# Batch 1 of a linear-attention and gated-MLP kernel: the first q division on GpSimd, the first v casts on ScalarE and VectorE, both q transposes ahead of the kv products

## The chip, the cores and the metric

The kernel runs on one core of a Trainium2 chip. The metric is the device time of one execution in microseconds; lower is better.

Names: TensorE (PE in the profile, PEld for its weight loads), VectorE (DVE), ScalarE (ACT), GpSimd (POOL), SyncE's DMA queue (SPq). One row of a trace view reads: start in us, length in us, engine, line of the program, operation, out<-in, shapes, count; in brackets, how long the engine stood idle before it and what ended that. Tile names: Eq is the exp of q, qz its sum and then 1/sum, tp the transposed q in PSUM and qT its copy in SBUF, va the cast v, Ek the exp of k, kvn the scaled kv, acc an output product and o its store, h a hidden product.

## The reference, cut to what matters

```python
def _attn_ref(q, k, v):                     # 8 batches, 8 heads, 576 rows, 64 columns
    q_s = np.exp(q - np.max(q, axis=-1, keepdims=True))
    q_s = q_s / (np.sum(q_s, axis=-1, keepdims=True) + 1e-09)
    k_s = np.exp(k - np.max(k, axis=2, keepdims=True))
    k_s = k_s / (np.sum(k_s, axis=2, keepdims=True) + 1e-09)
    kv = np.einsum('bhsd,bhse->bhde', k_s, v)
    return np.einsum('bhsd,bhde->bhse', q_s, kv)

def _moe_ref(x, w_in, w_out, beta):         # 4608 x 512, 512 x 2048, 2048 x 512
    h = x @ w_in
    g = h * (1.0 / (1.0 + np.exp(-beta * h)))
    return g @ w_out
```

## The kernel before: the parts that matter

The order of instructions on each engine is the order in which the program emits them; engines wait for each other by semaphores. Output products (`b_mm(n)`: n matmuls with w_out) are the filler that TensorE does between the pieces of batch 1's attention.

```python
def eq_sum(b, g):                           # VectorE
    nc.vector.tensor_reduce(qz[b][:, g], Eq[b][:, g], axis=AX.X, op=ALU.add)
    nc.vector.reciprocal(qz[b][:, g], qz[b][:, g])

def eq_div(b, g, eng):                      # 128 x 1024 bf16, in place, times 1/sum
    eng.tensor_tensor(Eq[b][:, g], Eq[b][:, g],
        qz[b][:, g].unsqueeze(3).to_broadcast((P, 2 * NT, 2, D)), ALU.mult)
# eq_exp, ek_exp: exp on ScalarE.  eq_t: 8 transposes on TensorE.  eq_out: their copy to SBUF.
# ev_cast(b, g, c, eng, t0, t1): v from f32 to bf16, 64 columns for each t (9 in all).
# ekv_mm: 18 kv products.  ekv_rk, ekv_norm: reciprocal and scaling of kv, half VectorE, half ScalarE.
# x_group: 4 products of q and kv.  unit_mm: hidden products (w_in) of the next chunk.

def batch_1():
    b_mm(32)
    eq_exp(1, 0)
    eq_exp(1, 1)
    eq_sum(1, 0)
    eq_div(1, 0, nc.vector)
    for c in range(2):
        ek_exp(1, 0, c)
    b_mm(6)
    ev_cast(1, 0, 1, nc.scalar, 0, 4)
    b_mm(14)
    eq_sum(1, 1)
    eq_t(1, 0, "X0", None)
    ev_cast(1, 0, 0, nc.gpsimd)
    ev_cast(1, 0, 1, nc.gpsimd, 4, KT9)
    eq_div(1, 1, nc.vector)
    for c in range(2):
        ek_exp(1, 1, c)
    b_mm(3)
    ekv_mm(1, 0, ("H0", "H1"))
    b_mm(1)
    eq_t(1, 1, "H2", None)
    ekv_rk(1, 0)
    ekv_norm(1, 0, (nc.vector, nc.scalar))
    eq_out(1, 0, nc.vector)
    ...                                     # v casts of the second half, cut
    eq_out(1, 1, nc.vector)
    b_mm(4)
    x_group(1, (0,), ["X0", "H0"])
    ekv_mm(1, 1, ("X1", "K"))
    ...                                     # as in both kernels, cut
```

The softmax here doesn't subtract the row's maximum and nothing guards it: scores larger than these inputs give would overflow.

## Time and profile before

| | before |
|---|---|
| time, median | 283.3 us (283.21 to 283.47) |
| profiled execution, span | 283.72 us, 282.0 us |
| TensorE busy | 276.2 us, 98% |
| batch 1's first exp starts (q has landed) | 36.84 us |
| hidden products of the next chunk start | 47.52 us |
| from there to the end | 234.5 us |

How to read it: TensorE is busy nearly throughout, so what counts is where it stands still. The one long stretch in which the chain of waits leaves TensorE after the loads at the start is batch 1, and the prediction below shows that chain line by line. Two moments of the trace: **q**, the start of the first exp of batch 1 on ScalarE, and **h**, the start of the hidden products of the next chunk on TensorE.

### The profile page before, as it was taken

Reading aid. Unit: us, or ns where it says so; the run is one execution under the profiler, and the core shown is the slowest. Engines: PE = TensorE matmul, PEld = TensorE weight load, DVE = VectorE, ACT = ScalarE, POOL = GpSimd, SP = SyncE. Lnnn points to the kernel's source line nnn. Section 1 sums busy time; section 2 is a strip of 40 time slices with the busy share of each in tenths; the row PEclk is TensorE's granted clock in tenths of the full one; section 3 lists DMA queues with packets and bytes.
Section 4 is the critical chain, followed back from the end, with each engine's and each line's share of the span. In section 5 each row is a group of like instructions: output and inputs, shape, how many; then the busy total and the mean of one; then the engine's idle time right before and its main releaser. Section 6 shows DMA issues by size and latency. Waiting matters only on the chain.

```text
span 282.0 us, 4639 instructions
## 1 busy us (share of the span) xinstructions
PE 276.2 (98%) x1692; PEld 136.3 (48%) x1692; DVE 155.7 (55%) x283; ACT 168.3 (60%) x280; POOL 70.1 (25%) x119
## 2 busy tenths in 40 slices
PE   7999999999999999999999999999999999999995
PEld 3545444445454445444544444444444444444444
DVE  2838369977865485638564766466453333444401
ACT  4757368867965587457854785478454544444411
POOL 3358731450631054104510361027000000000000
DMA  7999999879699917990599069904200200031112
GB/s 235 377 391 406 389 384 357 296 140 365 172 212 355 197 38 180 365 220 37 136 342 263 37 140 296 297 24 111 78 37 2 76 37 37 2 76 37 40 74 74
DMA packets 51559, 51.69 MB, mean 183 GB/s; under 512 B 21068, under 2 KB 41932, under 8 KB 51536
## 3 DMA queue, kind: packets, MB, share of 16 engines
q1 hardware_dynamic: 51360, 51.33, 60.9%
q8 instruction: 13, 0.21, 0.3%
q14 instruction: 10, 0.08, 0.1%
q10 hardware_dynamic: 144, 0.07, 0.1%
q0 software_dynamic: 32, 0.01, 0.0%
HBM read 38.28 MB, written 9.44 MB: 169 GB/s over the span
## 4 chain that ended last, share of the span: by engine, by line
PE 84%; DMA 11%; DVE 2%; SPq 1%; ACT 0%; issue 0%; POOL 0%; ACTq 0%
PE acc L509 40%; PE h L457 39%; DMA wo<-in_moe_w_out_dram 4%; DMA q<-in_q_dram 4%; DMA wi<-in_moe_w_in_dram 3%; PE kv L384 2%; PE x L408 2%; DVE Eq L205 1%; DVE qz L201 1%; SPq L105 1%; ACT Eq L194 0%; SPq L117 0%; PE xt L422 0%; POOL w_in_b L161 0%; PE kv L259 0%
## 5 line engine op out<-in xcount | busy, mean ns | idle before, releaser
L471 DVE SCALAR_TENSOR_TENSOR g<-th,h 128x512 bf16<-128x512 bf16 x144 | 97.2, 685 | 94.1 <-ACT th L469 93.9
L469 ACT ACTIVATE th<-h,beta_h 128x512 bf16<-128x512 f32 x144 | 97.2, 688 | 85.1 <-PE h L457 81.5
L509 PE MATMUL acc<-w_out_b,g 128*128 128x512 bf16 (+2 forms) x608 | 145.5, 368 | 0.0
L457 PE MATMUL h<-xT,w_in_b 128*128 128x512 bf16 x512 | 128.4, 379 | 0.0
L457 PEld LDWEIGHTS <-w_in_b 128*128 128x128 bf16 x576 | 64.9, 113 | 61.3 <-POOL w_in_b L161 0.5
L509 PEld LDWEIGHTS <-g 128*128 128x128 bf16 x608 | 56.9, 98 | 63.9 <-issue 2.5
L315 POOL TENSOR_TENSOR Eq<-Eq,qz 128x512 bf16<-128x512 bf16 x24 | 25.1, 1049 | 84.4 <-issue 41.0
L538 ACT ACTIVATE o<-acc 128x512 f32<-128x512 f32 x34 | 20.0, 591 | 8.9 <-PE acc L509 8.9
L161 POOL TENSOR_SCALAR_AFFINE_SELECT va<-v 128x256 bf16<-128x256 f32 (+3 forms) x55 | 21.4, 425 | 13.9 <-DMA v<-in_v_dram 13.7
L355 ACT ACTIVATE Ek<-k 128x640 bf16<-128x640 f32 x24 | 17.6, 735 | 0.0
L457 PE MATMUL h<-xTt,w_in_b 128*128 128x512 bf16 x64 | 16.4, 379 | 0.0
L313 DVE TENSOR_REDUCE qz<-Eq 128x8 f32<-128x512 bf16 x24 | 16.2, 675 | 0.0
L305 ACT ACTIVATE Eq<-q 128x512 bf16<-128x512 f32 x24 | 14.6, 622 | 0.0
L582 PE MATMUL warm<-zf 128*128 128x512 f32 (+1 forms) x14 | 9.6, 824 | 1.5 <-DVE zf L549 1.5
L201 DVE TENSOR_REDUCE qz<-Eq 128x16 f32<-128x1024 bf16 x4 | 4.9, 1215 | 10.9 <-ACT Eq L194 10.9
L166 DVE CAST xT<-x 128x512 bf16<-128x512 f32 x15 | 10.3, 684 | 0.6 <-PE x L408 0.5
L161 POOL TENSOR_SCALAR_AFFINE_SELECT w_in_b<-wi 128x512 bf16<-128x512 f32 x15 | 9.2, 629 | 4.0 <-DMA wi<-in_moe_w_in_dram 3.8
L152 ACT CAST xT<-x 128x512 bf16<-128x512 f32 x17 | 9.7, 578 | 0.7 <-PE x L408 0.5
L194 ACT ACTIVATE Eq<-q 128x1024 bf16<-128x1024 f32 x4 | 4.2, 1057 | 9.7 <-DMA q<-in_q_dram 9.7
L341 POOL TENSOR_TENSOR Et<-Et,zt 128x512 bf16<-128x512 bf16 x4 | 4.2, 1041 | 21.0 <-DVE zt L340 15.6
L161 POOL TENSOR_SCALAR_AFFINE_SELECT w_out_b<-wo 128x1024 bf16<-128x1024 f32 x8 | 8.3, 1039 | 1.9 <-DMA wo<-in_moe_w_out_dram 1.8
L408 PE MATMUL x<-qT,kvn 64*64 64x512 bf16 x64 | 5.9, 391 | 0.5 <-ACT xT L152 0.5
(53 smaller groups left out, 78.9 us busy)
## 6 DMA issues: line engine op xcount, KB each, us to landing
q<-in_q_dram SPq DMA_DIRECT2D x16, 512.0 KB, 5.7
out_dram<-o SPq DMA_DIRECT2D x31, 256.0 KB, 3.1
k<-in_k_dram SPq DMA_DIRECT2D x24, 320.0 KB, 7.2
v<-in_v_dram SPq DMA_DIRECT2D x24, 320.0 KB, 7.6
wo<-in_moe_w_out_dram SPq DMA_DIRECT2D x8, 512.0 KB, 10.4
wi<-in_moe_w_in_dram SPq DMA_DIRECT2D x6, 512.0 KB, 9.4
k<-in_k_dram SPq DMA_DIRECT2D x4, 576.0 KB, 8.9
v<-in_v_dram SPq DMA_DIRECT2D x6, 288.0 KB, 8.7
```

The lines of the kernel that those rows point to most:

```text
L161: nc.gpsimd.affine_select(out=dst, in_=src, pattern=[[0, n]], base=0, channel_multiplier=0, compare_op=ALU.is_equal, fill=fill0,)
L166: eng.tensor_copy(dst, src)
L305: nc.scalar.activation(by_pair(Eq[b], m).rearrange("p t h d -> p h t d"), ld["q", b, hf][:, a : a + 2, :].rearrange("p h (t d) -> p h t d" ...
L313: nc.vector.tensor_reduce(z, e, axis=AX.X, op=ALU.add)
L315: nc.gpsimd.tensor_tensor(e, e, z.unsqueeze(3).to_broadcast((P, NT, 2, D)), ALU.mult)
L355: nc.scalar.activation(Ek[b][:, :, h0:h1, :].rearrange("p t h d -> p h t d"), ld["k", b, hf][:, a : a + h1 - h0, :].rearrange("p h (t d) - ...
L408: nc.tensor.matmul(xps[b, 2 * g + c][o, :], kvn[b][r, j, :], qT[b][r, g, a] if b < EARLY else qT[b][r, :, j, :], start=True, stop=True,)
L457: nc.tensor.matmul(hs[n, i][:], w_in_b[:, kt, blk * CH + r : (blk + 1) * CH : 4], rhs_a(n, kt), start=(kt == 0), stop=(kt == KT - 1),)
L469: nc.scalar.activation(th[:], h[:], ACTF.Tanh, scale=beta_h[:, i // 4, i % 4 : i % 4 + 1])
L471: nc.vector.scalar_tensor_tensor(out=g[:], in0=th[:], scalar=1.0, in1=h[:], op0=ALU.add, op1=ALU.mult)
L509: nc.tensor.matmul(acc[n, st][:, c0:c1], gs[n, j][:, min(st, 3) * P : (min(st, 3) + 1) * P], w_out_b[:, j, c0:c1], start=(j == 0), stop=(j ...
L538: nc.scalar.activation(o[:], acc[n, st][:], ACTF.Copy, scale=0.5)
```

## The change

Its intent: VectorE did four long things in a row (sum, division, sum, division), and the second transposes waited for the last. The change gives the first division to GpSimd, gives GpSimd's v casts of the first half to ScalarE and VectorE in exchange, and puts both transposes ahead of the first kv products, which now need VectorE's cast.

```diff
-        eq_div(1, 0, nc.vector)
+        eq_div(1, 0, nc.gpsimd)
         for c in range(2):
             ek_exp(1, 0, c)
+        eq_sum(1, 1)
+        eq_div(1, 1, nc.vector)
         b_mm(6)
-        ev_cast(1, 0, 1, nc.scalar, 0, 4)
-        b_mm(14)
-        eq_sum(1, 1)
+        ev_cast(1, 0, 0, nc.scalar)
+        ev_cast(1, 0, 1, nc.vector)
+        b_mm(16)
         eq_t(1, 0, "X0", None)
-        ev_cast(1, 0, 0, nc.gpsimd)
-        ev_cast(1, 0, 1, nc.gpsimd, 4, KT9)
-        eq_div(1, 1, nc.vector)
+        eq_out(1, 0, nc.vector)
         for c in range(2):
             ek_exp(1, 1, c)
-        b_mm(3)
-        ekv_mm(1, 0, ("H0", "H1"))
         b_mm(1)
         eq_t(1, 1, "H2", None)
+        ekv_mm(1, 0, ("H0", "H1"))
         ekv_rk(1, 0)
         ekv_norm(1, 0, (nc.vector, nc.scalar))
-        eq_out(1, 0, nc.vector)
         ev_cast(1, 1, 0, nc.gpsimd)
-        ev_cast(1, 1, 1, nc.vector, 0, 3)
-        ev_cast(1, 1, 1, nc.scalar, 3, 6)
-        ev_cast(1, 1, 1, nc.gpsimd, 6, KT9)
+        ev_cast(1, 1, 1, nc.scalar, 0, 4)
+        ev_cast(1, 1, 1, nc.gpsimd, 4, KT9)
         eq_out(1, 1, nc.vector)
-        b_mm(4)
+        b_mm(5)
```

## The prediction

> **What bounds the kernel now.** I began with the page: the busy shares, then the chain of waits that ended last.
>
> ```profile
> PE 276.2 (98%) x1692; PEld 136.3 (48%) x1692; DVE 155.7 (55%) x283; ACT 168.3 (60%) x280; POOL 70.1 (25%) x119
> ...
> PE 84%; DMA 11%; DVE 2%; SPq 1%; ACT 0%; issue 0%; POOL 0%; ACTq 0%
> ```
>
> TensorE is busy for 98% of the span and carries 84% of the chain. The only stage in which another engine carries it for long, after the loads of the start, is the one that the change edits: batch 1's softmax and kv products, between the 52 output products that begin at 29.19 us and the hidden products of the next chunk, at 47.52 us. So the second view is the chain of waits between 36 and 54 us (start, length, what):
>
> ```profile
> 26.33 10.49 DMA q<-in_q_dram
> ...
> 36.84 1.07 ACT Eq L194
> ...
> 37.93 1.23 DVE qz L201
> ...
> 39.47 1.22 DVE Eq L205
> 40.70 1.14 DVE qz L201
> ...
> 42.15 1.24 DVE Eq L205
> 43.38 0.05 issue
> 43.43 0.62 PE tp L217 x8
> 44.05 0.86 PE acc L509 x4
> 44.91 0.66 PE x L408 x4
> 45.57 0.62 PE kv L259 x18
> 46.20 0.97 PE acc L509 x4
> 47.17 0.42 PE x L408 x4
> 47.59 5.30 PE h L457 x24
> ```
>
> Batch 1's q lands at 36.82 us, and from then VectorE does sum, division, sum, division in a row. The second division ends at 43.37 us and holds the second group of transposes. From 43.43 us on TensorE is on the path, and from 47.52 us it hardly stops: whatever the start of the hidden products moves by, the end moves by.
>
> How much is there to win? Between 29.19 and 47.52 us, 18.33 us, TensorE issues 64 output products at 0.216 us (52 of them show as one stretch of 11.39 us, the last of them 0.38 us: 11.01/51), two groups of transposes at 0.45, two kv groups at 0.62 and two x groups at 0.42 (the undisturbed one of the chain): 13.82 + 0.90 + 1.24 + 0.84 = 16.80 us. The holes are thus **about 1.5 us, 0.5% of the kernel**: 0.4 before the first transposes (ready at 40.42, started at 40.85), 0.55 before the second (42.88 to 43.43), 0.1 before and 0.24 inside the first x group (ScalarE's scaled kv), and some 0.2 in tenths. No reordering of this stage alone can reach 2%.
>
> **What the Trainium skill says.** "GPSIMD Engine Reference", section "Elementwise — side-by-side cycle accounting", puts a two-input tensor_tensor on GpSimd at about 2.6 cycles an element and about twice VectorE's time. The trace agrees roughly:
>
> ```profile
> L315 POOL TENSOR_TENSOR Eq<-Eq,qz 128x512 bf16<-128x512 bf16 x24 | 25.1, 1049 | 84.4 <-issue 41.0 <-DVE qz L314 28.7 <-PE acc L509 11.7
> L205 DVE TENSOR_TENSOR Eq<-Eq,qz 128x1024 bf16<-128x1024 bf16 x4 | 5.0, 1258 | 0.1
> ```
>
> 512 columns take 1.05 us on GpSimd, while VectorE does 1024 in 1.22 to 1.26. "SBUF — State Buffer", section "Who interferes with whom", says that a VectorE instruction with two SBUF inputs contends with a GpSimd instruction that reads SBUF, and that the loser blocks until the other is done; a tensor_reduce does not contend. This matters, since the change puts VectorE's second division beside GpSimd's first. Batch 0 shows a trace of it: of the four L205 divisions, 3 take 1224 ns, and the one that begins while GpSimd casts takes 1357.
>
> ```profile
> L205 DVE TENSOR_TENSOR Eq<-Eq,qz x4: 1224/1224/1357, 7.3 to 42.1; 128x1024 bf16<-128x1024 bf16 x4
> 9.98 1.36 DVE L205 TENSOR_TENSOR Eq<-Eq,qz 128x1024 bf16<-128x1024 bf16 x1
> 9.59 0.67 POOL L161 TENSOR_SCALAR_AFFINE_SELECT va<-v 128x576 bf16<-128x576 f32 x1 [6.09 <-DMA v<-in_v_dram]
> ```
>
> GpSimd's record ends at 10.26 us, the division loses 0.13 us, to 10.11: that fits a block if the cast has read its last input 0.15 us before its record ends. In batch 1 GpSimd's first v cast also starts at 40.62 us, just when the division of 39.47 us hands over to the next VectorE instruction. So I take the block as likely (about 2 in 3), not sure.
>
> **The change part by part.** The order of instructions on each engine shows that only batch 1 moved; TensorE, ScalarE and the sync queue keep their number of rows, VectorE and GpSimd have one less each.
>
> 1. First division, VectorE to GpSimd. The sum's reciprocal is done at 39.44 us; GpSimd follows such a release by 0.15 to 0.19 us (division at 50.09 after a reciprocal ended at 49.90). 1024 columns at 1.02 to 1.05 us per 512 give 2.05 us (estimate): 39.6 to **41.65**, against 40.69 before. Cost: 0.96 us later.
> 2. First transposes now follow 54 output products instead of 52, free at 40.42 + 0.43 = 40.85; they wait for GpSimd, start at about 41.77 and end at 42.22. The hole grows from 0.4 to about 0.9 us.
> 3. VectorE, freed of the first division, sums the second half at once: 39.47 to 40.7, reciprocal to 40.96, division due at 41.0. Unblocked it would end at 42.2 (1.17 earlier than the 43.37 of before). Blocked until GpSimd's reads end at about 41.5 it ends at **42.7**.
> 4. One output product (to 42.44), then the second transposes: 42.82 to 43.27, with a hole of 0.4.
> 5. v casts. ScalarE's full half replaces its 256 columns: 0.67 us (batch 0's 576-column cast) from 41.1 to 41.8, in place of 0.41; its two stores and the exp of the second half shift by about 0.1 to 0.3. VectorE's 576-column cast is new: the 0.353 us of its 192-column cast plus 384 columns at 1.05 ns (its reduces: 1215 less 675 ns for 512 columns) make 0.75 us, from 42.65 to **43.4**. (A w_in cast of 512 columns took only 0.428 us; if this one goes at that pace, the step is 0.25 us shorter. I keep the pace of the same odd layout, 64 columns each time.) It now gates the kv products, where before GpSimd (41.84) and ScalarE did.
> 6. First kv products: 43.4 to 44.05 (hole 0.15). Five output products to 45.13. Meanwhile VectorE copies the transposed q (0.69 us, to 44.05), takes reciprocals to 44.3 and scales kv to 44.95; ScalarE scales its half to 45.0. So the x group starts at about 45.15 without the hole inside and ends at 45.57.
> 7. Second kv products at **45.57**, against 45.51 before: +0.06. After them the order is the same: four output products, x group near 47.15, hidden products at 47.58. The v casts of the second half (GpSimd 320 columns in place of 192, ScalarE 256, VectorE none) end by 45.4 and are beside the path.
>
> Sum with the block: holes of 0.9 + 0.4 + 0.15 + tenths, as many as before. The two holes have moved earlier and merged, not shrunk: **+0.05 us**. Without the block step 3 ends at 42.2, the second transposes follow without a hole, kv starts at 43.0, and ScalarE's scaling of kv (44.8) and then its cast (45.2) limit: kv group two near 45.25, **-0.25 us**.
>
> **The rivals.**
> - No block between the divisions, or a partial one: -0.25 us, 283.05. For it: only one slowed division of four shows the block. Against it: the page of the skill and the 0.13 us.
> - GpSimd is slower than twice its 512-column time, or VectorE wins the port first and GpSimd waits for it: each tenth on the division is a tenth on the whole chain. Up to +0.6 us, 283.9. Against it: the 24 L315 divisions average 1.049 us beside VectorE's work.
> - The stage shrinks to its TensorE work because the holes all close: -1 us or more, 282.3 or less. Against it: step 1 makes the first operand 0.96 us later, and only two more output products, 0.43 us, are put in front of it.
> - Loads: q, k, v of batch 2 wait on GpSimd's weight casts and on the queue, not on batch 1, so they don't move. If q of batch 1 lands later or earlier by some tenths in a given run, both kernels move alike.
>
> **Range and chances.** 0.65 x 0.05 - 0.25 x 0.25 + 0.1 x 0.5 comes to +0.02 us. From 283.3 us, I predict 283.3, and 282.7 to 283.9 as the range: the rivals of -0.25 and +0.6, the few tenths of my hand schedule, and the 0.26 us spread of the three runs before. Faster or slower by over 2% (5.7 us) is beyond the 1.5 us that the stage has to give, and a loss of that size would need a division some 5 us long: 1% each.
>
> **What would show it.** GpSimd's L205 division: 2.05 us, ending near 41.65 (step 1). VectorE's L205: over 1.5 us long or begun only at about 41.5 if blocked, 1.22 us from 41.0 if not (step 3). The wait of the first transposes on GpSimd, about 0.9 us (2). VectorE's 576-column cast: 0.75 us, ending last before kv (5). Hidden products of the next chunk from 47.3 to 47.6 us (7), and everything after shifted by that difference. I am wrong if the division on GpSimd is not near 2 us, if the kv products wait for something else, or if the part after 47.5 us changes its own length.

## The result, and the profile after

The changed kernel takes 283.16 us (median of 4, 282.99 to 283.23) against 283.34 (median of 4, 283.21 to 283.47) for the kernel before. Ratios in this text are the mean time of one kernel's fast runs over that of the other's of the same rounds, so not quite the ratio of these medians: 0.9993, with a 95% interval of 0.9975 to 1.001. A second set of five rounds gave 1.0001 (0.9986 to 1.0015). The change is worth nothing that the clock can show.

The profile page of the changed kernel, busy shares and the chain that ended last (28 matmul records are missing from this trace, 1664 of 1692, so its TensorE time is not compared):

```profile
PE 273.0 (97%) x1664; PEld 136.6 (49%) x1692; DVE 155.5 (55%) x282; ACT 168.6 (60%) x280; POOL 71.7 (25%) x118
...
PE 83%; DMA 13%; ACT 1%; issue 1%; SPq 1%; ACTq 0%
```

The spans of the two profiled executions differ by 0.6 us (282.0 and 281.4), which looks like a gain. It is not: in this execution q landed 0.6 us earlier. The chain of waits of the changed kernel between 26 and 54 us (start, length, what):

```profile
39.21 1.26 ACT Ek L230 x2
40.47 0.56 ACT va L152
41.03 0.99 ACT o L538 x2
...
42.09 0.61 PE tp L217 x8
42.70 0.06 issue
42.76 0.69 PE kv L259 x18
43.45 0.16 issue
43.61 1.03 PE acc L509 x4
44.63 0.34 PE x L408 x4
44.98 0.62 PE kv L259 x18
45.60 0.97 PE acc L509 x4
46.57 0.42 PE x L408 x4
46.99 3.58 PE h L457 x16
```

The chain is led through ScalarE's store, which ended last, at 42.00 us, before the transposes of 42.09, and from there back to k's landing. The profile puts a wait down to what came last; the transposes need VectorE's division and ScalarE's exp, not that store, and the division ended at 41.94. That VectorE is the real releaser is shown by an experiment below (the first undo), where TensorE stands idle for 1.67 us and the transposes start 0.14 us after VectorE's division has ended; here it is 0.15 us. (This view starts a piece only where the one before it ends, 46.99 for the hidden products; **h** is their start in the rows of the trace, 46.92.) What VectorE, GpSimd and TensorE did, from the trace in order of time:

```profile
36.21 1.06 ACT L194 ACTIVATE Eq<-q 128x1024 bf16<-128x1024 f32 x1 [5.38 <-DMA q<-in_q_dram]
38.79 1.22 DVE L201 TENSOR_REDUCE qz<-Eq 128x16 f32<-128x1024 bf16 x1
38.96 1.90 POOL L205 TENSOR_TENSOR Eq<-Eq,qz 128x1024 bf16<-128x1024 bf16 x1 [3.16 <-DVE qz L202]
40.33 1.61 DVE L205 TENSOR_TENSOR Eq<-Eq,qz 128x1024 bf16<-128x1024 bf16 x1
41.87 0.74 DVE L166 CAST va<-v 128x576 bf16<-128x576 f32 x1
42.76 0.69 PE L259 MATMUL kv<-va,Ek 64*128 64x131 bf16 x18
46.92 1.92 PE L457 MATMUL h<-xT,w_in_b 128*128 128x512 bf16 x8
```

GpSimd needs 1.90 us for what VectorE does in 1.22. The sum beside it keeps its 1.22 us, but VectorE's own division, which starts 0.53 us before GpSimd's ends, takes 1.61. And the kv products start 0.15 us after VectorE's cast has ended. Measured from q, this is the same length of stage as before:

| | q | h | h - q | h to the end of the span |
|---|---|---|---|---|
| before | 36.84 | 47.52 | 10.68 | 234.5 |
| after | 36.21 | 46.92 | 10.71 | 234.5 |

### The profile page after: what moved, and what is told of

Read it like the earlier page. It is cut to its first block, busy times and chain, and to the rows that moved or that the text cites. A ratio compares the mean times of both kernels' runs of the same rounds, so it can differ in the third digit from the quotient of the medians.

```text
span 281.4 us, 4613 instructions
## 1 busy us (share of the span) xinstructions
PE 273.0 (97%) x1664; PEld 136.6 (49%) x1692; DVE 155.5 (55%) x282; ACT 168.6 (60%) x280; POOL 71.7 (25%) x118
## 4 chain that ended last, share of the span: by engine, by line
PE 83%; DMA 13%; ACT 1%; issue 1%; SPq 1%; ACTq 0%
PE acc L509 40%; PE h L457 39%; DMA k<-in_k_dram 7%; DMA wo<-in_moe_w_out_dram 3%; DMA wi<-in_moe_w_in_dram 2%; PE kv L384 2%; PE x L408 1%; PE kv L259 0%; ACT Ek L230 0%; ACT o L538 0%; SPq L105 0%; SPq L117 0%; PE xt L422 0%; PE tp L217 0%; ACT va L152 0%
## 5 line engine op out<-in xcount | busy, mean ns | idle before, releaser
L509 PE MATMUL acc<-w_out_b,g 128*128 128x512 bf16 (+2 forms) x590 | 142.6, 368 | 1.8 <-issue 1.3
L161 POOL TENSOR_SCALAR_AFFINE_SELECT va<-v 128x256 bf16<-128x256 f32 (+2 forms) x53 | 21.1, 436 | 10.0 <-DMA v<-in_v_dram 9.8
L230 ACT ACTIVATE Ek<-k 128x576 bf16<-128x576 f32 x8 | 5.0, 675 | 2.3 <-DMA k<-in_k_dram 2.3
```

What stands on the lines that cost most here:

```text
L161: nc.gpsimd.affine_select(out=dst, in_=src, pattern=[[0, n]], base=0, channel_multiplier=0, compare_op=ALU.is_equal, fill=fill0,)
L509: nc.tensor.matmul(acc[n, st][:, c0:c1], gs[n, j][:, min(st, 3) * P : (min(st, 3) + 1) * P], w_out_b[:, j, c0:c1], start=(j == 0), stop=(j ...
```

## The experiments

The theory: the stage hangs on q's landing, and the chain behind it (GpSimd's division, VectorE's blocked division, VectorE's cast, kv products) is as long as the old one, by coincidence of sizes and not because the moved parts are hidden. The rivals: TensorE's own stream sets h, and the parts are hidden; or the change closes holes and is worth the 0.6 us between the two profiled spans.

The two controls, the undone division and the cast ahead of the division ran on one chip, with a median of 283.27 us for the kernel before; the other four on another, with 283.24. All outputs were correct.

### Two controls: both kernels again, unchanged

```diff
(no edit)
```

> A control: the kernel before, unchanged, for a second trace. Let q be the moment at which batch 1's first half of q starts its exp on ScalarE (36.84 us in the trace of before, 36.21 in that of after). Theory: the stage's end, the start of the next chunk's hidden products, lies a fixed 10.7 us after q in both kernels (47.52 - 36.84 and 46.92 - 36.21), and the span ends 234.5 us after that; so q may land between 36 and 37.2 us, and the hidden products follow at q + 10.7 within 0.15. Rival: q's landing does not matter, TensorE's own stream does, and the hidden products stay at 47.5 us wherever q lands.

> A control: the changed kernel, unchanged, with five rounds. Theory: the change is worth nothing, ratio 0.9985 to 1.0005, hidden products at q + 10.7 within 0.15 us (as in before), VectorE's second division again 1.6 us and GpSimd's 1.9 us. Rival (the change really closes holes and is worth the 0.6 us by which the two profiled spans differ): ratio 0.998 and hidden products at q + 10.1 where q lands as it did before.

Measured: the kernel before had q at 36.22 us this time and h at 46.89: h - q is 10.67, and its span 281.4 us, exactly the span of the profile after. The changed kernel had q at 36.17 and h at 46.88, 10.71 apart, ratio 1.0001 (0.9986 to 1.0015). The two rows of the kernel before:

```profile
36.22 1.06 ACT L194 ACTIVATE Eq<-q 128x1024 bf16<-128x1024 f32 x1 [6.09 <-DMA q<-in_q_dram]
46.89 1.92 PE L457 MATMUL h<-xT,w_in_b 128*128 128x512 bf16 x8
```

So q's landing varies from execution to execution, and in the kernel before h moved with it (0.63 us for 0.62); the 0.6 us between the first two spans was that. The rival of a real gain falls. For a stage set by TensorE's stream: in the first trace of before the output products began 0.39 us later than in the second (29.19 and 28.80 us), and h went with q. In those of after they began at 29.51 and 29.60, but q differs by only 0.04 us, too little to tell. What tells there is the waiting: in both traces the second transposes start 0.15 us after VectorE's division has ended, and the kv products 0.14 to 0.15 us after its cast. TensorE is not far behind, though: 29.51 plus the prediction's 16.80 us of work is 46.31, only 0.6 us before h. And since q, k and v landed at nearly the same distances from each other in these four traces, a fixed h - q does not single out q among the loads; in after it is VectorE's row, without a gap from the first sum (37.30) to the end of the cast (42.61), that leads back to q.

### Undo the division's move alone

```diff
-        eq_div(1, 0, nc.gpsimd)
+        eq_div(1, 0, nc.vector)          # in the changed kernel
```

> The changed kernel with the first division back on VectorE, nothing else undone: the casts and the transposes stay moved. Theory: VectorE then does sum, division, sum, division and the 576-column cast in a row, the cast ends at q + 7.2 in place of q + 6.4, the first kv products start at q + 7.3 in place of q + 6.55, and the hidden products move to about q + 11.4: 0.7 us longer than after, ratio to before about 1.0025. VectorE's two divisions take 1.22 us each, since GpSimd reads nothing meanwhile. Rival (where the division runs is hidden by TensorE's output products): the same as after within 0.15 us.

Measured: 284.09 us, ratio 1.0039 (1.0018 to 1.0060), h - q = 48.63 - 37.13 = 11.50, 0.79 over after, as the theory had it (0.7); the medians of the same rounds, 284.09 and 283.31, say 0.78. The profiled execution was one of the longer of its kernel (284.86 us), with q late; h - q takes that out. VectorE's rows and TensorE's in this trace:

```profile
42.43 1.23 DVE L205 TENSOR_TENSOR Eq<-Eq,qz 128x1024 bf16<-128x1024 bf16 x1
43.57 0.75 DVE L166 CAST va<-v 128x576 bf16<-128x576 f32 x1
43.80 0.61 PE L217 MATMUL tp<-ident,Eq 128*128 128x128 bf16 x8 [1.67 <-DVE Eq L205]
44.47 0.69 PE L259 MATMUL kv<-va,Ek 64*128 64x131 bf16 x18
```

With GpSimd idle the second division takes 1.23 us, but it begins at q + 5.30 instead of q + 4.12, and TensorE stands 1.67 us before the second transposes. The division is not hidden by the output products. Given the other two parts, its move is worth 0.8 us.

### The division's move alone, in the kernel before

```diff
-        eq_div(1, 0, nc.vector)
+        eq_div(1, 0, nc.gpsimd)          # in the kernel before
```

> The kernel before with its first division on GpSimd and nothing else changed, so GpSimd still has the first half's v casts behind it. Times from q, the start of the first exp on ScalarE. Theory: GpSimd divides until q + 4.65, VectorE's division is blocked to q + 5.75 (1.6 us long), and GpSimd's two v casts come after that: they start at q + 5.6 in place of q + 3.8 and end at q + 6.8. The first kv products start at q + 6.9 in place of q + 5.2 and the hidden products at about q + 11.5 in place of q + 10.7: 0.8 us longer than before, ratio 1.003. Rival (the division's move is what pays, and the moved casts and transposes do nothing): as after, q + 10.7, ratio 0.9995.

Measured: 284.02 us, ratio 1.0022 (1.0001 to 1.0042), h - q = 47.91 - 36.74 = 11.17, 0.49 over before; the direction as expected, the size in the trace 0.3 smaller. The medians, 284.02 and 283.24, are 0.78 us apart, so the size stays between the two. GpSimd, VectorE and TensorE in order of time:

```profile
39.49 1.90 POOL L205 TENSOR_TENSOR Eq<-Eq,qz 128x1024 bf16<-128x1024 bf16 x1 [3.18 <-DVE qz L202]
40.87 1.60 DVE L205 TENSOR_TENSOR Eq<-Eq,qz 128x1024 bf16<-128x1024 bf16 x1
41.35 1.65 POOL L161 TENSOR_SCALAR_AFFINE_SELECT va<-v 128x576 bf16<-128x576 f32 x1
43.05 0.87 PE L259 MATMUL kv<-va,Ek 64*128 64x131 bf16 x18 [0.33 <-POOL va L161]
```

The two engines hold each other up in turn: the division waits for GpSimd's division, and GpSimd's cast then waits for the division, 1.65 us in place of the 0.67 that the same cast takes elsewhere. I had put the end of GpSimd's two casts at q + 6.8; they ended at 43.41, q + 6.67, and the kv products had begun at q + 6.31 on the first cast alone. So moving the division without the casts loses.

### The kv products ahead of the second transposes again

```diff
         b_mm(1)                          # in the changed kernel
-        eq_t(1, 1, "H2", None)
         ekv_mm(1, 0, ("H0", "H1"))
+        eq_t(1, 1, "H2", None)
```

> The changed kernel with the first kv products ahead of the second transposes again, as before; division and casts stay moved. Theory: kv waits for VectorE's 576-column cast, which ends at q + 6.4, in either order; the transposes, 0.45 us, no longer fill that wait but follow kv, so all from the x group on comes 0.4 us later: hidden products at q + 11.1, ratio to before about 1.0015, 0.4 us over after. Rival (the order does not matter because the x group waits for kv's scaling and not for TensorE): hidden products at q + 10.7 as after.

Measured: 283.91 us, ratio 1.0017 (0.9997 to 1.0036), h - q = 47.65 - 36.49 = 11.16, 0.45 over after. The kv products start at q + 6.55 as in after, since they wait for the cast in either order; TensorE stands 1.00 us before them, and the 0.45 us of the transposes then follow:

```profile
43.04 0.69 PE L259 MATMUL kv<-va,Ek 64*128 64x131 bf16 x18 [1.00 <-DVE va L166]
```

The clock's interval just reaches 1 (medians 283.91 and 283.24); the shift by 0.45 in the trace is what carries this.

### VectorE's cast ahead of its division, kv ahead of the second transposes

```diff
         eq_sum(1, 1)                     # in the changed kernel
-        eq_div(1, 1, nc.vector)
         b_mm(6)
         ev_cast(1, 0, 0, nc.scalar)
         ev_cast(1, 0, 1, nc.vector)
+        eq_div(1, 1, nc.vector)
         b_mm(16)
         eq_t(1, 0, "X0", None)
-        eq_out(1, 0, nc.vector)
         for c in range(2):
             ek_exp(1, 1, c)
-        b_mm(1)
-        eq_t(1, 1, "H2", None)
         ekv_mm(1, 0, ("H0", "H1"))
         ekv_rk(1, 0)
         ekv_norm(1, 0, (nc.vector, nc.scalar))
+        eq_out(1, 0, nc.vector)
         ...                              # v casts of the second half, unchanged
+        b_mm(2)
+        eq_t(1, 1, "H2", None)
         eq_out(1, 1, nc.vector)
-        b_mm(5)
+        b_mm(4)
```

> The changed kernel with VectorE's v cast ahead of its division, and the first kv products ahead of the second transposes (two output products between them). Theory of the shared read port: VectorE's second division, which took 1.61 us beside GpSimd's, now begins after GpSimd's has ended (q + 4.65) and takes 1.22 us; the cast[...] runs beside GpSimd's division at its 0.74 us and leaves that at 1.90. The kv products no longer wait for the division: they start at about q + 5.5 in place of q + 6.55, the x group at q + 7.9 in place of q + 8.35, and the hidden products at q + 10.4 in place of q + 10.7, as long as TensorE's own work (16.8 us after its first output product) isn't later: 0.3 us less than after, ratio to before 0.998 to 0.9995. Rival (the division took 1.6 us for another reason, such as its place behind the reciprocal): it takes 1.6 us here too. Rival (ScalarE's scaled kv sets the x group anyway): hidden products stay at q + 10.7.

Measured: 282.83 us, ratio to before 0.9983 (0.9971 to 0.9996), h - q = 46.88 - 36.59 = 10.29, 0.42 less than after. The rows that decide between the reasons for the long division:

```profile
39.34 1.90 POOL L205 TENSOR_TENSOR Eq<-Eq,qz 128x1024 bf16<-128x1024 bf16 x1 [3.19 <-DVE qz L202]
41.08 0.75 DVE L166 CAST va<-v 128x576 bf16<-128x576 f32 x1 [0.41 <-DMA v<-in_v_dram]
41.75 1.22 DVE L205 TENSOR_TENSOR Eq<-Eq,qz 128x1024 bf16<-128x1024 bf16 x1
41.98 0.69 PE L259 MATMUL kv<-va,Ek 64*128 64x131 bf16 x18
43.76 0.61 ACT L279 ACTIVATE kvn<-kv,rks 64x64 bf16<-64x64 f32 x2
44.46 0.41 PE L408 MATMUL x<-qT,kvn 64*64 64x512 bf16 x4
```

GpSimd's division ended at 41.24 us. VectorE's began after that and took 1.22 us; in after, overlapping, it took 1.61. Data and shape are alike. Its predecessor is not: here it follows the cast, in after the reciprocal. But with q loaded earlier (below) and with the division undone (above) it follows the reciprocal, as in after, without a GpSimd division beside it, and takes 1.23 us. So the overlap is the cause. The overlap of cast and GpSimd's division is only 0.16 us here, and neither is longer for it; that is weak evidence that this cast does not contend. The kv products start at q + 5.39 in place of q + 6.55. The x group then starts at 44.46 us, right after ScalarE's scaled kv (43.76 plus 0.61), which waits behind the second half's exp and so for k's landing. But TensorE is no earlier: its four output products from 43.50 us, at 0.216 us each, also end at about 44.36. Two limits thus lie close together, and 1.16 us at the kv products become 0.42 at h; which of the two is the harder one no run tells. **This is the version that beats both kernels**: by 0.17% of before, with an interval below 1, and by its median against 283.31 for the changed kernel in the same rounds. The edit moves the cast, the kv products and a copy together, so the gain is that of the whole edit.

### q loaded earlier, in both kernels

```diff
     for j0 in range(0, NJ, 2):
+        if j0 == 14:
+            load_q(1, 0)
         load_w_out(j0)
...
-            for hf in range(2):
-                load_q(1, hf)
+            load_q(1, 1)
```

> The changed kernel with the first half of batch 1's q loaded ahead of the last w_out block in place of behind it; the same bytes in another order. The first exp should start about 1.3 us earlier, near 34.9 us; the second half of q, k and v land as they did, the last w_out cast 1.3 us later, still before its product. Theory (the stage hangs on q's landing): the first sum is out of the way, GpSimd's division ends near 39.1 us, before VectorE's division begins at 40.3, which is thus not blocked and takes 1.22 us; the cast ends at 42.2 in place of 42.6, kv follows, and the hidden products start 0.4 us earlier, near 46.45 us: ratio to before 0.998 to 0.9995. TensorE's own work allows no more than 0.5. Rival (VectorE's sum or v's landing sets kv): hidden products at 46.9 as after.

> The kernel before with the same earlier load of q. Theory: VectorE's two divisions end near 38.4 and 41.5 us in place of 40.0 and 42.7, so both groups of transposes start without a wait; but in this order ScalarE stores a third output and does the second half's exp ahead of its scaling of kv, which ends at 44.5 us and holds the x group as it did: the hidden products move by 0.1 us at most, to 46.8, ratio 0.999 to 1.0005. Rival (q's landing alone sets the stage's end in before, by VectorE's chain): 0.6 us or more earlier, ratio 0.998 or less.

Measured, the changed kernel first: h came at 46.94 us, not at the expected 46.45 but where the rival had it. The expectation took the second half of q, k and v to land as in the trace of after; they landed 0.4 us later (second exp at 38.10 in place of 37.70, the second half's k exp at 42.59 in place of 42.22). So h is counted from the second half's exp, a measure chosen after the result: before 38.34 and after 37.70 give h minus it of 9.18 and 9.22, and here it is 8.84, which is 0.38 less, the size that the theory gave. The clock: 283.03 us, ratio 0.9987 (0.9967 to 1.0006). The last w_out cast, expected to be in time, was not: TensorE waited 0.55 us for it before the stage, but the second transposes and the kv products still started 0.14 and 0.15 us after VectorE's division and cast. GpSimd's division ended at 39.93, before VectorE's began at 40.74, and VectorE's took 1.23 us:

```profile
38.03 1.90 POOL L205 TENSOR_TENSOR Eq<-Eq,qz 128x1024 bf16<-128x1024 bf16 x1 [0.36 <-DVE qz L202]
40.74 1.23 DVE L205 TENSOR_TENSOR Eq<-Eq,qz 128x1024 bf16<-128x1024 bf16 x1
```

In the kernel before the same earlier load is worth nothing: second exp at 37.69, h at 46.88, 9.19 apart against 9.18; 283.31 us, ratio 0.9999 (0.9978 to 1.0021). Both transposes started without a wait there, and the x group still waited for ScalarE's scaled kv, which ended at 44.47. VectorE's second division ended 4.03 us after the second exp's start, in before 5.03, and h did not move. So before has two chains of about the same length side by side, VectorE's and ScalarE's. (Here too the division overlapped with GpSimd, with its casts: it took 1.40 us, and the 320-column cast behind it 1.30 in place of 0.45.) The clock's intervals of these two hold 1; the difference of 0.38 rests on the traces, one of each.

## Why the prediction was right

The forecast, 283.3 us in a range of 282.7 to 283.9, holds 283.16, and the sum of +0.05 us for the stage was measured as +0.03 (10.71 less 10.68). That the sum is so near is luck in part, as steps 1 and 2 show. The steps, with predicted times counted from the q of before (36.84) and measured ones from the q of after (36.21):

| step | predicted | measured |
|---|---|---|
| 1. GpSimd's division: length, end | 2.05, q + 4.81 | 1.90, q + 4.65 |
| 2. first transposes start | q + 4.93 | q + 4.95 |
| 3. VectorE's division, blocked: end | q + 5.86 | 1.61 long, q + 5.73 |
| 4. second transposes start | q + 5.98 | q + 5.88 |
| 5. VectorE's cast: length, end | 0.75, q + 6.56 | 0.74, q + 6.40 |
| 6. kv products, x group start | q + 6.56, q + 8.31 | q + 6.55, q + 8.35 |
| 7. second kv products, h | q + 8.73, q + 10.74 | q + 8.70, q + 10.71 |

- **The block (2 in 3 in the prediction) is there.** VectorE's division takes 1.61 and 1.63 us in two traces of after and 1.60 with the division's move alone (1.63 with the order put back), all beside GpSimd's division, and 1.22 or 1.23 in the three kernels in which GpSimd does not work at that time. It ends where the prediction put it: by the lost time, 0.14 us before the end of GpSimd's record.
- **One size was off in step 1:** 1.90 us, not 2.05, since twice the 512-column time counts the fixed part twice. Steps 3 to 5 carry it (0.13, 0.10 and 0.16 us early); from step 6 on it is gone, because the kv products started 0.15 us after the cast, where the prediction allowed nothing. Two errors cancel.
- **One reading was off in step 2:** the hole of 0.9 us before the first transposes. The wait for GpSimd that the prediction named as its sign did not come in after. The output products began at 29.51 in place of 29.19 us, and q landed 0.63 earlier, so TensorE was busy until 41.16, 0.30 us past the end of GpSimd's division (40.86). That the transposes start at q + 4.95 against the predicted 4.93 is therefore luck; it did not matter, since the next transposes wait for VectorE. With the division's move alone, where q came later and the products began earlier (28.94), TensorE did wait for GpSimd, 1.12 us. The start of the output products goes with what happened in batch 0, whose code is the same in all ten traces: they begin at 28.80 to 29.19 us in the four traces in which GpSimd's first v cast starts ahead of VectorE's second division (9.58 to 9.74 us), and at 29.42 to 29.65 in the six in which it comes second (9.97 to 10.40) and is held up. Both traces of before are of the first kind, both of after of the second.
- **Each partial version that was run loses, and the whole breaks even.** By the traces, the division alone costs 0.49 us (its casts wait behind it); casts and order without the division cost 0.82 over before (11.50 less 10.68); division and casts without the order cost 0.48 (11.16 less 10.68). The casts alone and the order alone were not run. The prediction said of the holes that they "moved earlier and merged, not shrunk". Between the first output product and h they did shrink in the traces, from 1.53 and 1.29 us in before to 0.61 and 0.48 in after (h less that start less 16.80), since the products began later; h - q stayed.
- **One chain was not seen.** The prediction took VectorE's row for what bounds the kernel before, and ScalarE's scaled kv for a hole of 0.24 us. The earlier q in the kernel before shows in its one trace that ScalarE's chain is as long: VectorE's became 1.0 us shorter, and h stayed.
- **The rivals.** "No block" at -0.25 us: the changed kernel with q early, in which nothing blocks, gained 0.38 by one trace, so the mechanism fits, and its size was somewhat larger. "GpSimd slower" did not come. "Holes all close" did not come in after; the version with the cast first gets 0.42 us of it. "Loads vary, both kernels alike": shown by the controls.

What stays open: no run tells what makes q land between 36.2 and 37.1 us in different executions of the same loads.

## What to carry to other kernels

Before moving a two-input elementwise operation to GpSimd, look at what VectorE does in that time: in these traces a two-input operation there waited for it (1.61 in place of 1.22 us), while a sum did not (1.22), so put a sum beside GpSimd and the two-input one after it. (A one-input cast was seen beside it for 0.16 us only.) When a profiled stage differs between two kernels by less than the landing of a load varies, measure the stage from that landing and profile the unchanged kernel a second time. When an edit has parts that each pay for another, try the parts apart; here all three partial versions lost, and the gain came with another order of VectorE's cast and division, moved together with the kv products.

## What the Trainium skill lacked or had wrong

- "SBUF — State Buffer", section "Who interferes with whom", says that a VectorE instruction with two SBUF inputs contends with GpSimd's reads, and that the one that comes second blocks fully. The traces agree in both directions, but it doesn't say how a profile shows it: the block is neither idle time nor a wait, it is inside the blocked instruction's recorded length (1.61 in place of 1.22 us). In batch 0 of the trace of after GpSimd is the one that loses, 1.39 us in place of 0.67, against the division that started before it (these two rows):

```profile
9.94 1.22 DVE L205 TENSOR_TENSOR Eq<-Eq,qz 128x1024 bf16<-128x1024 bf16 x1
10.30 1.39 POOL L161 TENSOR_SCALAR_AFFINE_SELECT va<-v 128x576 bf16<-128x576 f32 x1 [6.81 <-DMA v<-in_v_dram]
```

- The same section has the shared ports locked for the whole instruction. Reckoned from the lost time, the block ends about 0.14 us before the end of the holder's record: VectorE lost 0.39 us from 40.33, to 40.72, and GpSimd's record ended at 40.86; in batch 0 GpSimd lost 0.72 from 10.30, to 11.02, and VectorE's ended at 11.16. In the other overlaps of these traces the difference is 0.13 to 0.16 us too, however long the overlap. This assumes that a blocked instruction needs its whole undisturbed time after the block; if a part of it runs during the block, the block lasts longer. No run tells these apart, so the page is not shown wrong.
- "GPSIMD Engine Reference", section "Elementwise — side-by-side cycle accounting", gives about 2.6 cycles an element for a two-input tensor_tensor (measured in fp32) and calls it the floor of two inputs. Here, in bf16, 512 columns take 1.05 us and 1024 take 1.90: 1.66 ns for each further column, or 2.0 cycles at the page's 1.2 GHz, and about 0.2 us fixed (an estimate from these two lengths). The page has no bf16 figure.
- "VectorE: DVE Perf Modes", section "What auto-detection actually checks", lets one source and a destination in SBUF go at two elements a cycle if their outermost dimensions are both even or equal. A w_in cast of 512 columns took 0.428 us, the v cast of 9 times 64 columns 0.74. The v casts of 192 (in before) and 576 columns differ by 1.02 ns a column, while the w_in cast took 0.84 ns a column with its fixed part included, so the v cast went at the slower pace. The section doesn't say how rows that lie without a gap count: the 9 rows of the source do and may count as one run of 576, the 9 of the destination don't. Whether that is the cause no run here tells, so this is a gap and not an error.
